# A fixed TensorE order, one plain token tile, spread output products and paired value additions in a local-attention plus gated-MLP block

## The chip, the cores and the metric

The kernel runs on one core of one Trainium2 chip. The metric is the device time of one execution in microseconds (us); when a kernel is compared, several executions of both kernels are taken in turn on the same chip. The engines are called PE (TensorE, matmuls), PEld (the weight loads of TensorE, which overlap its matmuls), DVE (VectorE), ACT (ScalarE), POOL (GpSimd) and SP (SyncE). An engine name with a q (SPq) is that engine's instruction queue; it shows the issue of a transfer, not the transfer itself. L920 is line 920 of the kernel in question, so the same statement has another number in another kernel.

## The reference, cut to what matters

`x` has S = 2048 tokens of 512 features. Two branches read its layernorm. Branch A is attention with 32 heads of 16 features over a window of 8 keys, two tokens apart. Branch B is a gated MLP whose gate mixes tokens with a 2048 x 2048 matrix.

```python
xn = layernorm(x)
# A: 32 heads of 16, window of 8 keys, every second token
q, k, v = split(xn @ wqkv)                       # wqkv 512 x 1536
logits  = sum_d q[s] * k[s - 2*w] * scale        # w = 0..7, masked where s - 2*w < 0
o       = sum_w softmax(logits)[s, w] * v[s - 2*w]
a       = o @ wo                                 # wo 512 x 512
# B: gated MLP with a spatial matrix
z       = gelu(xn @ w_in)                        # w_in 512 x 1792
z1, z2  = z[:, :896], layernorm(z[:, 896:])
g       = w_sp @ z2 + b_sp[:, None]              # w_sp 2048 x 2048
b       = (z1 * g) @ w_out                       # w_out 896 x 512
y       = x + a + b
```

## The kernel before

The program is written as a list of tasks. Each task says what it reads and writes, and a list scheduler in Python, which runs when the kernel is built, puts the tasks of each engine into an order and places the semaphores. The kernel has two stages. In the first 100 us the projections run (q, k, v, z1, z2), DVE multiplies queries with keys, and TensorE sums these products with matmuls against a 0/1 matrix `E8`. In the second stage the spatial product g is computed for four tiles of 512 tokens. For six of seven groups of 128 features it uses seven products of half-size blocks in place of eight (a Winograd form of Strassen's scheme): 256-column matmuls, which need sums of z2 and differences of weights made on DVE. The seventh group is a plain product of 512 columns. Beside this, DVE multiplies attention weights with values and adds them up over the window ("value products"), a transfer transposes the result (`OT`), and TensorE makes the output blocks.

Three kinds of large transfer:

- *Weight transposes*: a DMA transpose of 2 MB of `w_sp` for each token tile, issued by SP, into two slots `wT0` and `wT1`.
- *Value loads*: 1.15 MB (1152 KB in the profile) into one of two buffers `Ve`, issued by POOL, two for each token tile.
- *Output transposes*: small DMA transposes of the attention output from `On` into `OT`, also issued by SP.

Parts, with cuts marked by `...`:

```python
# --- buffers: lay(base, ...) without "base =" starts at the same place as the next line
base = lay(base, ("Sn", 3 * NK * 384))
...
lay(base, ("Ve", 9216), ("wT1", WSL), ("Vs", 4096), ("On", 512), ("xres", 1024), ("yout", 1024), ("wo0", 512))
base = lay(base, ("QT", 4096), ("KT", 8 * (512 + KP)), ("pb", NPB * 4096))
```

So the value buffers lie over queries and keys (and the first part of `pb`), and the second weight slot lies over the products `pb` of the logits: the second weight transpose can start only when the last of these products has been summed.

```python
def prod_reduce(j, c):                       # wave j of 512 tokens, c = 0..3
    ...                                      # DVE: pb[s_] = q * k, 128 x 4096
    if c < 3:
        return
    def mm(t):                               # one piece of 32 matmuls for all four c
        for wh in range(2):
            for cc in range(4):
                sc = (s_ - 3 + cc) % NPB
                for g in range(4):
                    last = t.matmul(PC(32 * g * PR + 3072 + 512 * wh, [[1, 512]], 32),
                                    AC(off["E8"] + 32 * cc, [[1, 32]]),
                                    AC(off["pb"] + 4096 * sc + 2048 * wh + 128 * g, [[512, 4], [1, 128]]),
                                    start=(cc == 0), stop=(cc == 3))
        return last
    T("pe", mm, reads=[("pb", i) for i in range(4)] + ["E8"], writes=["psl"], ...)

def ld_wT(tc, after=()):                     # the weight transpose (L920)
    r_ = tc % 2
    dma("sp", lambda e: e.dma_start_transpose(AC(WT[r_], [[512, NB], [1, 512]]),
        B_w_sp[512 * tc: 512 * tc + 512, :]), 512 * S * 2, ("wT", r_), reads=after,
        writes=[("wB", r_, q) for q in range(4)], name="wT%d" % tc, xbar=True)

def pv_block(b):                             # value products of one block of 128 tokens
    ...
    if q < 2:
        dma("pool", ...)                     # value load into Ve[par] (L1100)
    # DVE: Vs = Ve * attn (4096), then Vs += halves of 2048, 1024, and On = 512 + 512
    ...
    dma("sp", lambda e: e.dma_start_transpose(AC(off["OT"] + 512 * b, [[128, 4], [1, 128]]),
        A("On", 512, 512 * so)), ...)        # the output transpose (L1118)

plain(0); t_sums(0); ld_wT(1)                # written as three lines
for tc in range(NJ):
    for i in range(3):
        prod7(i, tc)                         # seven products, two feature groups each
    for q in qord:
        pv_block(4 * tc + q)
    if tc + 1 < NJ:
        if tc + 2 < NJ:
            ld_wT(tc + 2)
        plain(tc + 1)
        bdiff(tc + 1)
        t_sums(tc + 1)
    for q in qord:
        out_block(4 * tc + q, ...)           # attention part first, then the MLP part
```

Of the kernel before, what the change touches and what calls it, by code (L numbers as in the profile page):

```python
# [9 lines left out]
class Task:  # L10
    __slots__ = ("eng", "fn", "reads", "writes", "est", "name", "dma", "deps", "idx",
                 "start", "end", "eng_end", "count", "tok", "clock", "prio", "tbl", "margin")


class Plan:
# [37 lines left out]
    def add(self, eng, fn, reads=(), writes=(), est=100.0, name="", dma=None, prio=None, tbl=None, margin=0.0):  # L53
# [30 lines left out]
        t.deps = deps  # L84
        for k in t.reads:
            if k not in t.writes:
                self.readers.setdefault(k, []).append(t)
# [6 lines left out]
    def schedule(self, lookahead=64, slack=120.0, dma_bw=300.0, xbar_bw=190.0,  # L94
# [31 lines left out]
        while remaining:  # L126
            best = None
            for e in ENGS:
# [6 lines left out]
                for t in pl:  # L135
                    ok = True
                    ready = 0.0
                    for d in t.deps:
                        if d.end is None:
                            ok = False  # L140
                            break
                        r = d.end + lat(d, t)
                        if r > ready:
                            ready = r
# [66 lines left out]
    def emit(self, nc, block, sems, chan_sems):  # L211
# [32 lines left out]
        def run_engine(e):  # L244
            def body(eng):
                known = {}
                for t in self.order[e]:
                    need = {}
                    dl = [d for d in t.deps if known.get(d.tok[0], 0) < d.tok[1]]
# [57 lines left out]
    fill0=2,  # L307
)


def build_kernel(nc, A_x, A_wqkv, A_wo, B_x, B_w_in, B_w_sp, B_b_sp, B_w_out, out, report=False, sched_kw=None,
# [36 lines left out]
    def lay(base, *items):  # L348
        for name, n in items:
# [6 lines left out]
    base = lay(base, ("Sn", 3 * NK * 384))  # L356
# [4 lines left out]
    lay(base, ("Ve", 9216), ("wT1", WSL), ("Vs", 4096), ("On", 512), ("xres", 1024), ("yout", 1024), ("wo0", 512))  # L361
# [6 lines left out]
               ("bbc", S), ("cb", 2048), ("wo1", 1536))  # L368
    WO = (off["wo0"], off["wo1"], off["wo1"] + 512, off["wo1"] + 1024)
# [15 lines left out]
    with ExitStack() as es:  # L385
# [3 lines left out]
        bdt = es.enter_context(nc.sbuf_tensor("bdt", [128, 512], F32))  # L389
# [33 lines left out]

        def q_off(c, j):
            return off["QT"] + (c * S + 512 * j if not True else 2048 * (j % 2) + 512 * c)
# [11 lines left out]
        for s_ in range(2):  # L437
            R1(("On", s_), "On", 512)
# [10 lines left out]
        R1("Vs", "Vs", 4096)  # L449
        for s_ in range(2):  # L450
# [17 lines left out]
        for b in range(NB):  # L468
            R(("xnT", b), "sb", [(off["xnT"] + dc * S + 128 * b, off["xnT"] + dc * S + 128 * b + 128)
                                 for dc in range(4)])  # L470
            R1(("OT", b), "OT", 512, 512 * b)
            R1(("z2", b), "z2", FH, FH * b)
        R1("w_in1", "w_in1", 4 * FH)
# [24 lines left out]
        def c_dve(n, mode=1.0):  # L498
            return 130.0 + n / (0.96 * mode)

        T = plan.add
# [221 lines left out]
        def prod_reduce(j, c):  # L723
# [9 lines left out]
            if R2:  # L733
                if c < 3:
                    return

                def mm(t):
                    last = None
                    for wh in range(2):
                        for cc in range(4):  # L740
                            sc = (s_ - 3 + cc) % NPB
                            for g in range(4):
                                last = t.matmul(
                                    PC(32 * g * PR + 3072 + 512 * wh, [[1, 512]], 32),
                                    AC(off["E8"] + 32 * cc, [[1, 32]]),
                                    AC(off["pb"] + 4096 * sc + 2048 * wh + 128 * g, [[512, 4], [1, 128]]),
                                    start=(cc == 0), stop=(cc == 3))
                    return last
                T("pe", mm, reads=[("pb", i) for i in range(4)] + ["E8"], writes=["psl"],
                  est=8 * 232.0 + 190, name="red%d" % j, margin=cfg.get("m_red", 800.0))  # L750
                return

            def mm(t):
                last = None
                for blk in range(4):
                    t0, ts = tok(4 * j + blk)
                    for w in range(8):
                        last = t.matmul(ps[:, 3072 + blk * 256 + w * 32 + 8 * c: 3072 + blk * 256 + w * 32 + 8 * c + 8],
                                        AC(off["pb"] + 4096 * s_ + 512 * w + t0 - 512 * j, [[ts, 128]]), E8,
                                        start=True, stop=True)  # L760
                return last
            T("pe", mm, reads=[("pb", s_), "E8"], writes=["psl"], est=32 * 25 + 30, name="red%d_%d" % (j, c),
              margin=cfg.get("m_red", 800.0))

# [90 lines left out]
        def z1_group(fc, j):  # L855
            k = next_bank()
# [41 lines left out]
        def s_sums(k0, k1):  # L898
# [7 lines left out]
            zk = [("z2", b) for b in range(2 * k0, 2 * k1)]  # L906
            a11, a12, a21, a22 = z_(0), z_(FH), z_(384), z_(FH + 384)
            for nm, o_, x_, y_, op, rd, wr in (
                    (1, sn(0), a21, a22, ALU.add, zk, [("Sn", 1, k) for k in range(k0, k1)]),
                    (2, sn(1), sn(0), a11, ALU.subtract, zk + [("Sn", 1, k) for k in range(k0, k1)],  # L910
                     [("Sn", 2, k) for k in range(k0, k1)]),
                    (3, a21, a11, a21, ALU.subtract, [], zk),
                    (4, sn(2), a12, sn(1), ALU.subtract, zk + [("Sn", 2, k) for k in range(k0, k1)],
                     [("Sn", 4, k) for k in range(k0, k1)])):
                T("dve", (lambda o_, x_, y_, op: lambda v: v.tensor_tensor(o_, x_, y_, op))(o_, x_, y_, op),
                  reads=rd, writes=wr, est=c_dve(384 * n, 2.0), name="S%d_%d" % (nm, k0))

        def ld_wT(tc, after=()):
            r_ = tc % 2
            dma("sp", lambda e: e.dma_start_transpose(  # L920
# [18 lines left out]
        for j in range(NJ):  # L939
            bl = range(4 * j, 4 * j + 4)  # L940
            for b in bl:
                if b >= 8:
                    ld_x(b)
            if j == 1:
                ld_win1(after=[("xn", 2)])
            for b in bl:
                ln_block(b)
            if j == 0:
                setup_masks()
                for b in bl:  # L950
                    z2_block(b)
            if j == 1:
# [280 lines left out]
```

## Time and profile before

| Kernel before | value |
|---|---|
| time, median of 3 runs | 275.12 us (272.65 to 275.19) |
| span of the profiled run | 270.6 us |
| PE busy | 233.2 us (86%) |
| DVE busy | 207.4 us (77%) |
| idle PE after 104 us | about 31 us |

The page of the profile gives each engine's busy time, and then the span in 40 equal slices, where a digit is the busy share in tenths. The last strip is the clock that the throttle granted to TensorE, in tenths of full speed.

```profile
PE 233.2 (86%) x1493; PEld 138.7 (51%) x1511; DVE 207.4 (77%) x257; ACT 144.1 (53%) x305; POOL 57.3 (21%) x110
...
PE   6999999999999999998005998289999877999696
...
PEclk9999999999999999999855999989999999999979
```

TensorE is nearly full for the first 19 slices; then there is a hole of two slices, with the granted clock down to a half, and smaller holes to the end. The groups of waits say what ended the idle time of an engine: engine and line, the releaser, the total in us, how often, and the longest.

```profile
PE ps L1020 <- DMA arena<-in_B_w_sp_dram: 16.0, 1, 16.0
...
DVE arena L936 <- DMA arena<-in_B_w_sp_dram: 13.0, 1, 13.0
...
PE ps L1058 <- ACT ps L999: 6.4, 6, 1.4
...
PE ps L1141 <- DMA arena<-arena: 5.2, 1, 5.2
```

TensorE's largest wait, and DVE's, is one single transfer of spatial weights. L1058 are the 256-column matmuls; they wait 6.4 us in all for ACT, which hands one product's sum over to the next (a hand-over, below). L1141 is the attention part of an output block, which waits 5.2 us for an output transpose. The timeline around the large wait has start, duration (of the issue, for a transfer), engine, line and operation, and in brackets the idle time before it:

```profile
110.02 0.60 POOL L1100 DMA_DIRECT2D arena<-vscr  x1 [18.42 <-DVE arena L730]
...
113.59 0.55 POOL L1100 DMA_DIRECT2D arena<-vscr  x1 [2.98 <-PE ps L743]
114.07 17.23 SPq L920 DMA_TRANSPOSE arena<-in_B_w_sp_dram  x1
...
125.27 0.54 POOL L1100 DMA_DIRECT2D arena<-vscr  x1 [10.07 <-DVE arena L1107]
...
136.47 3.71 SPq L1118 DMA_TRANSPOSE arena<-arena  x1
140.22 10.06 SPq L920 DMA_TRANSPOSE arena<-in_B_w_sp_dram  x1
...
145.14 2.34 PE L1020 MATMUL ps<-arena 128*128 128x512 bf16 x5 [16.00 <-DMA arena<-in_B_w_sp_dram]
```

Both value loads of the first token tile and the second weight transpose are issued within 4.1 us, and a third value load follows at 125.27. TensorE gets its weights at 145 us. The times from issue to landing of the three weight transposes after 100 us (L920):

```profile
DMA to landing us min/median/max: 9.5/12.1/30.6
```

The same of the 16 output transposes (L1118):

```profile
DMA to landing us min/median/max: 2.4/3.0/8.7
```

The transpose in the gap is the one that took 30.6 us.

### The profile page before, as it was taken

Reading aid. Unit: us, or ns where it says so; the run is one execution under the profiler, and the core shown is the slowest. Engines: PE = TensorE matmul, PEld = TensorE weight load, DVE = VectorE, ACT = ScalarE, POOL = GpSimd, SP = SyncE. Lnnn points to the kernel's source line nnn. Section 1 sums busy time; section 2 is a strip of 40 time slices with the busy share of each in tenths; the row PEclk is TensorE's granted clock in tenths of the full one; section 3 lists DMA queues with packets and bytes.
Section 4 is the critical chain, followed back from the end, with each engine's and each line's share of the span. In section 5 each row is a group of like instructions: output and inputs, shape, how many; then the busy total and the mean of one; then the engine's idle time right before and its main releaser. Section 6 shows DMA issues by size and latency. Waiting matters only on the chain.

```text
span 270.6 us, 3910 instructions
## 1 busy us (share of the span) xinstructions
PE 233.2 (86%) x1493; PEld 138.7 (51%) x1511; DVE 207.4 (77%) x257; ACT 144.1 (53%) x305; POOL 57.3 (21%) x110
## 2 busy tenths in 40 slices
PE   6999999999999999998005998289999877999696
PEld 2544454454444444787002884048487356578543
DVE  4696897896999899689405899689990999989900
ACT  2796689689898875367100533136344154344323
POOL 4556754506100200200000002220121001320000
PEclk9999999999999999999855999989999999999979
DMA  6997920102190003599999723857982252642021
GB/s 221 358 275 142 249 42 31 49 0 80 30 280 2 0 0 107 211 231 177 127 186 234 170 39 76 235 164 161 273 249 49 77 156 62 208 104 58 19 58 61
DMA packets 59266, 35.53 MB, mean 131 GB/s; under 512 B 49644, under 2 KB 56684, under 8 KB 58224
## 3 DMA queue, kind: packets, MB, share of 16 engines
q1 hardware_dynamic: 53856, 18.29, 32.7%
q0 software_dynamic: 3312, 15.22, 19.3%
q10 hardware_dynamic: 2080, 1.77, 2.0%
q8 instruction: 12, 0.20, 0.3%
q14 instruction: 6, 0.05, 0.1%
HBM read 19.01 MB, written 4.21 MB: 86 GB/s over the span
## 4 chain that ended last, share of the span: by engine, by line
PE 52%; DVE 24%; DMA 17%; issue 3%; ACT 3%; SPq 0%; POOL 0%; DVEq 0%; ACTq 0%
DMA arena<-in_B_w_sp_dram 11%; PE ps L704 10%; PE ps L861 9%; PE ps L844 9%; DVE arena L1107 8%; PE ps L1058 5%; PE ps L684 5%; PE ps L1146 5%; DMA arena<-arena 4%; PE ps L1020 4%; DVE arena L1109 4%; PE ps L1141 3%; DVE arena L936 2%; DVE arena L1112 2%; DVE arena L1079 2%
## 5 line engine op out<-in xcount | busy, mean ns | idle before, releaser
L1058 PE MATMUL ps<-arena 128*128 128x256 bf16 x672 | 75.8, 273 | 6.4 <-ACT ps L999 6.4
L1058 PEld LDWEIGHTS ps<-arena 128*128 128x128 bf16 x672 | 65.1, 98 | 17.7 <-ACT ps L999 8.4
L1107 DVE TENSOR_TENSOR arena<-arena 128x4096 bf16<-128x4096 bf16 x16 | 36.6, 2291 | 1.2 <-DMA arena<-vscr 0.7
L730 DVE TENSOR_TENSOR arena<-arena 128x4096 bf16<-128x4096 bf16 x16 | 35.9, 2278 | 0.0
L936 DVE TENSOR_TENSOR arena<-arena 128x2048 bf16<-128x2048 bf16 x16 | 19.5, 1221 | 21.1 <-DMA arena<-in_B_w_sp_dram 13.0
L999 ACT ACTIVATE arena<-ps 128x256 bf16<-128x256 f32 (+1 forms) x28 | 11.4, 412 | 40.9 <-PE ps L1020 25.1
L1152 ACT ACTIVATE arena<-ps 128x512 bf16<-128x512 f32 (+2 forms) x17 | 9.7, 572 | 43.9 <-PE ps L1146 37.5
L1020 PE MATMUL ps<-arena 128*128 128x512 bf16 x60 | 15.0, 402 | 16.1 <-DMA arena<-in_B_w_sp_dram 16.0
L1146 PE MATMUL ps<-arena 128*128 128x512 bf16 (+2 forms) x119 | 28.5, 382 | 0.0
L704 PE MATMUL ps<-arena 128*128 128x512 bf16 x125 | 28.0, 379 | 0.3 <-ACT arena L871 0.2
L844 PE MATMUL ps<-arena 128*128 128x448 bf16 x128 | 25.7, 353 | 0.9 <-ACT arena L712 0.3
L1141 PE MATMUL ps<-arena 128*128 128x512 bf16 (+2 forms) x63 | 17.0, 393 | 8.9 <-DMA arena<-arena 5.2
L861 PE MATMUL ps<-arena 128*128 128x512 bf16 x109 | 24.2, 379 | 0.2
L1129 POOL DMA_DIRECT2D arena<-in_A_x_dram x16 | 8.6, 538 | 66.1 <-ACT ps L1136 38.2
L1146 PEld LDWEIGHTS ps<-arena 128*128 128x128 bf16 x119 | 13.5, 117 | 13.3 <-issue 3.2
L704 PEld LDWEIGHTS ps<-arena 128*128 128x128 bf16 x128 | 12.4, 98 | 15.3 <-issue 0.4
L1109 DVE TENSOR_TENSOR arena<-arena 128x2048 bf16<-128x2048 bf16 x16 | 19.5, 1221 | 0.4
L999 ACT ACTIVATE ps<-ps 128x256 f32<-128x256 f32 x36 | 13.1, 367 | 12.1 <-PE ps L1058 10.3
L849 ACT ACTIVATE arena<-ps 128x448 bf16<-128x448 f32 x32 | 17.2, 547 | 3.5 <-PE ps L844 1.8
L712 ACT ACTIVATE arena<-ps 128x1024 bf16<-128x1024 f32 x16 | 16.2, 1021 | 5.3 <-PE ps L704 5.3
L844 PEld LDWEIGHTS ps<-arena 128*128 128x128 bf16 x128 | 12.1, 98 | 13.1 <-ACT arena L671 1.0
L1020 PEld LDWEIGHTS ps<-arena 128*128 128x128 bf16 x64 | 6.5, 103 | 23.8 <-DMA arena<-in_B_w_sp_dram 15.9
(75 smaller groups left out, 296.7 us busy)
## 6 DMA issues: line engine op xcount, KB each, us to landing
arena<-vscr POOLq DMA_DIRECT2D x8, 1152.0 KB, 6.5
vscr<-arena POOLq DMA_DIRECT2D x16, 128.0 KB, 3.3
arena<-in_A_x_dram POOLq DMA_DIRECT2D x16, 128.0 KB, 3.3
arena<-in_A_x_dram SPq DMA_DIRECT2D x14, 128.0 KB, 7.3
out_dram<-arena POOLq DMA_DIRECT2D x12, 128.0 KB, 3.8
arena<-in_A_wqkv_dram SPq DMA_DIRECT2D x2, 512.0 KB, 7.9
arena<-in_B_w_in_dram SPq DMA_DIRECT2D x1, 896.0 KB, 7.9
arena<-in_B_w_out_dram SPq DMA_DIRECT2D x1, 896.0 KB, 5.0
```

What stands on the lines that cost most here:

```text
L704: last = t.matmul(bank(k + which), AC(off["wqk"] + 1024 * dc + col0, [[1, 128]]), AC(off["xnT"] + dc * S + 512 * j, [[1, 512]]), start=(dc ...
L730: T("dve", lambda v: v.tensor_tensor(pbv, qb, kb, ALU.mult), reads=rd, writes=[("pb", s_)], est=c_dve(4096, 2.0), name="prod%d_%d" % (j, c ...
L844: last = t.matmul(ps[:, 512 * k: 512 * k + HF], AC(off["xnT"] + dc * S + 128 * b, [[1, 128]]), AC(off["w_in2"] + FH * dc + c0, [[1, HF]]), ...
L861: lastm = t.matmul(bank(k), AC(off["w_in1"] + FH * dc + 128 * fc, [[1, 128]]), AC(off["xnT"] + dc * S + 512 * j, [[1, 512]]), start=(dc == ...
L936: T("dve", (lambda o_, x_, y_: lambda v: v.tensor_tensor(o_, x_, y_, ALU.subtract))(o_, x_, y_), reads=rd, writes=[wr], est=c_dve(NK * 256 ...
L999: T("act", lambda a: a.activation(out_, in_, ACTF.Copy), reads=reads, writes=writes, est=c_act(n), name=name)
L1020: last = t.matmul(bank(k), AC(off["z2"] + FH * sh + 128 * fc, [[1, 128]]), AC(WT[r_] + sh * 512, [[1, 512]]), start=False, stop=(sh == NB ...
L1058: last = t.matmul(half(bk), lh(k), rh(k), start=False, stop=(k == NK - 1), skip_group_check=True)
L1107: T("dve", lambda v: v.tensor_tensor(tv, iv, av, ALU.mult), reads=[("attn", j)] + rdv, writes=["Vs"], est=c_dve(4096, 2.0), name="pv%d" % ...
L1109: T("dve", lambda v: v.tensor_tensor(A("Vs", 2048), A("Vs", 2048), A("Vs", 2048, 2048), ALU.add), writes=["Vs"], est=c_dve(2048, 2.0), nam ...
L1141: t.matmul(po, AC(off["OT"] + 512 * tb + 128 * cc, [[1, 128]]), AC(WO[cc] + c0, [[1, n]]), start=False, stop=False, skip_group_check=True)
L1146: last = t.matmul(po, AC(off["z1T"] + fc * S + t0, [[ts, 128]]), AC(off["w_out"] + 512 * fc + c0, [[1, n]]), start=False, stop=(fc == FC - ...
```

## The change

The change writes TensorE's order by hand instead of leaving it to the scheduler (only the reductions of the logits and the transposes of x stay with the scheduler). The first token tile uses plain products only, so that its weights' differences and sums need not be made and there is work for TensorE while the second weights come. Output blocks and the plain products of the next tile are cut into slices that are placed in the gaps between the seven products. The value products of two blocks share their additions. The reduction of the logits becomes four pieces, the order of the projection waves changes, the value buffers get space of their own, output blocks do their MLP part first, output and residual transfers move from POOL's queue to ACT's, SP's transposes get a fixed order too, TensorE no longer waits on semaphores for its own earlier matmuls, the products read z2 by parts instead of as a whole, all of `wo` gets space of its own, and banks and scheduler constants change.

The core of the diff, with cuts marked:

```diff
+    def sequence(self, tasks):
+        for a, b in zip(tasks, tasks[1:]):
+            b.odeps.add(a)
...
-    def schedule(self, lookahead=64, slack=120.0, dma_bw=300.0, xbar_bw=190.0,
+    def schedule(self, lookahead=400, slack=120.0, dma_bw=300.0, xbar_bw=400.0,
...
-    base = lay(base, ("Sn", 3 * NK * 384))
-    lay(base, ("Ve", 9216), ("wT1", WSL), ("Vs", 4096), ("On", 512), ("xres", 1024), ("yout", 1024), ("wo0", 512))
+    base = lay(base, ("Ve", 9216))
+    lay(base, ("Sn", 3 * NK * 384), ("wT1", WSL), ("Vs", 4096), ("On", 1024), ("xres", 1024), ("yout", 1024))
...
-                T("pe", mm, reads=[("pb", i) for i in range(4)] + ["E8"], writes=["psl"],
-                  est=8 * 232.0 + 190, name="red%d" % j, margin=cfg.get("m_red", 800.0))
+                T("pe", mm, reads=[("pb", s_), "E8"], writes=["psl"],
+                  est=2 * 232.0 + 100, name="red%d_%d" % (j, c), margin=cfg.get("m_red", 800.0))
...
-            P(1, X, za(0), wb(0), z2all + [("wB", r_, 0)])
+            P(1, X, za(0), wb(0), za11 + [("wB", r_, 0)])
+            gap()
...                                            # two more gap() in each prod7
+        def pv_pair(j, par):
...
+            for n, nm in ((2048, "a"), (1024, "b"), (512, "c")):
+                o_ = two(0, n) if n > 512 else AC(off["On"], [[512, 2], [1, 512]])
+                T("dve", (lambda o_, n: lambda v: v.tensor_tensor(o_, two(0, n), two(n, n), ALU.add))(o_, n),
+                  reads=[] if n > 512 else ["Vs", ("Ve", par)], writes=["Vs", ("Ve", par)] if n > 512 else ["On"], ...)
+            return dma("sp", lambda e: e.dma_start_transpose(AC(off["OT"] + 2048 * j + 1024 * par, [[128, 8], [1, 128]]),
+                                                             A("On", 1024)), ...)
...
         for tc in range(NJ):
+            if tc == 0 and P0:                 # P0 = cfg["first_plain"]
+                for fc in (3, 4, 5, 0, 1, 2, 6):
+                    for n_, f_ in plain_slices(0, next_bank, (16,), fc):
+                        f_()
+                for n_, f_ in plain_slices(1, next_bank, (16,)):
+                    f_()
...
+            else:
+                pl = plain_slices(tc + 1, ob) if tc + 1 < NJ else []
+                oq = [out_slices(4 * (tc - 1) + q) for q in qord] if tc > 0 else [[], [], [], []]
+                q_ = oq[0] + oq[1] + pl + oq[2] + oq[3]
...                                            # gap() takes its share of q_
+                for i in range(3):
+                    prod7(i, tc, gap)
+            for par in range(2):
+                if tc > 0:
+                    ld_V(tc, par)
+                sp_seq.append(pv_pair(tc, par))
+                if par == 0 and tc + 2 < NJ:
+                    sp_seq.append(ld_wT(tc + 2))
...
+        plan.sequence(pe_seq)
+        plan.sequence(sp_seq)
```

## The prediction

> **What bounds the kernel now.** PE is 233.2 of 270.6 us busy (page; 86%), DVE 207.4 (77%). In the view by stretches PE is busy 96.5 of the first 100 us: the projections are PE-bound. After they end, at 104 us, PE idles 31 us, nearly all in waits:
> - 129.1 to 145.1 us: 16.0 us for the second token tile's spatial-weight transpose (groups of waits; DVE 13.0). It was issued only at 114.07: its space overlays the logits' product buffers, freed by the reduction at 113.2. Two value loads of 1.15 MB were issued at 110.0 and 113.6. It took 30.6 us to land; the median of the four is 10.9. After it seven matmuls start 0.43 us apart instead of 0.22: 1.5 us more. The Trainium skill, "TensorE: Matmul & The Clock Gate", Part 1, says that an idle TensorE drops to half clock; this trace agrees (granted clock 0.65 in the gap).
> - 5.2 us for a transposed attention output (170 to 175 us), then 4.5 us at 210-233 and 2.3 us before 256.9, where DVE is late; the chain runs on DVE from 210 to 256 us.
>
> **What changes.**
> - Tile 0 uses plain products: 168 matmuls of 256 columns out (measured pitch 0.110 us, 18.5 us), 96 of 512 in (0.216 us, 20.7 us): PE +2.3 us. DVE loses four weight differences (4 x 1.22) and three merges and multiplies (3 x 1.37), gains six multiplies of 0.42: -6.5 us.
> - Value products: additions of two blocks share an instruction; per pair 2 x (1.22+0.69+0.42) = 4.7 becomes 2.3+1.22+0.69 = 4.2 us (estimate); 8 pairs: -3.8 us.
> - Value buffers get their own space, so tile 0's loads go early, away from the weight transpose. That can go about 20 us earlier, and TensorE has 128 plain matmuls (27.7 us) to hide it.
> - Output and plain matmuls between the seven products cover ScalarE's 0.38 us hand-overs, which now stall PE 6.4 us in all. Output DMAs move from Pool to ACT, which has room (53%).
>
> **Sum.** The plain stage should start at about 107 us: 104.3, plus the fourth reduction (1.9), which came later before, plus small waits for the logits' products, which DVE must finish some 10 us earlier. Then 27.7 + 504 x 0.110 (55.4) + 32 x 0.216 (6.9) + 176 x 0.216 (38.0) = 128 us: 235 us. I add 5 us of waits where DVE (about 197 us in all) and PE run neck and neck, and 3 us for the last store: span 243. The reported time is 2 to 4 us above the span (272.3 against 270.6; median 275.1). I predict 246 us, 8 in 10 between 239 and 256: 10.5% faster. On the critical path: 17.5 us from the late transpose, some 10 from outputs and DVE waits. Chances: faster by over 2% 0.97, same 0.02, slower 0.01.
>
> **What would show it.** No PE wait over 3 us on spatial weights; second weight transpose issued before 100 us, landing in under 20; PE busy above 93%, its clock 1.0 from 10 us on; DVE about 197 us; a chain mostly PE; pair addition 2.3 us.
>
> **What would make it wrong.** TensorE's order is fixed, so one late operand stops everything behind it: logits' products late on DVE (PE waits at the 32-row matmuls), weight differences of tiles 1 to 3 late (waits at the 256-wide matmuls), or ACT evictions held behind a DMA waiting in its queue. The pair addition could lose its rate (over 3 us).

## The result

The kernel after takes 252.03 us (median of 4 runs, 249.21 to 253.45); the kernel before took 274.31 us in the runs beside it (272.65 to 275.19, 4 runs). The ratio is 0.9125, with a 95% interval of 0.9021 to 0.9229. Ratios in this document are the mean time of one kernel's fast runs over that of the other's fast runs of the same rounds, so they are not quite the ratio of the medians that are quoted beside them. Against the quick mode of the kernel before, which turns up in the experiments below (mean 264.6 us), the kernel after is about 5% faster (251.05 us in the second set). The 246.0 that was predicted is 6 us too low; the range of 239 to 256 holds the result.

The profiled run took 253.04 us. It is called slow by the rule that a run more than 1.5% above the kernel's fastest is slow (it is 1.54% above), but the four runs (249.21, 251.03, 253.04, 253.45) are a spread without a gap. A second trace of the same kernel from the second set of experiments (250.57 us) shows the same waits with other sizes, and is quoted beside it.

The page after, same parts:

```profile
PE 235.3 (94%) x1413; PEld 130.6 (52%) x1439; DVE 195.6 (78%) x228; ACT 142.6 (57%) x293; POOL 48.5 (19%) x82
...
PE   8799998999999999999999983999799989999994
...
PEclk9999999999999999999999996899999999999999
```

PE is busy as long as before, in a span that is 19 us shorter. One deep hole is left, in the 25th slice, with a lower clock behind it. The waits after:

```profile
DVE arena L1144 <- DMA arena<-arena: 10.9, 2, 6.1
...
PE ps L1042 <- DMA arena<-in_B_w_sp_dram: 4.8, 1, 4.8
...
PE ps L1187 <- DVE arena L1118: 1.4, 1, 1.4
```

The wait for spatial weights went from 16.0 to 4.8 us, and it is for another tile: the third, not the second. The output matmuls (L1187) no longer wait for an output transpose. In exchange DVE waits 10.9 us for output transposes before its paired additions (L1144), because they write the one buffer `On` that the transpose still reads. The timeline around the hole shows how this comes about:

```profile
116.29 1.25 SPq L1147 DMA_TRANSPOSE arena<-arena  x1
...
116.49 0.60 POOL L1124 DMA_DIRECT2D arena<-vscr  x1 [21.89 <-DVE arena L1144]
...
134.88 13.11 SPq L933 DMA_TRANSPOSE arena<-in_B_w_sp_dram  x1
138.17 0.55 POOL L1124 DMA_DIRECT2D arena<-vscr  x1 [21.08 <-DVE arena L1144]
148.03 10.16 SPq L1147 DMA_TRANSPOSE arena<-arena  x2
154.82 1.46 PE L1042 MATMUL ps<-arena 128*128 128x512 bf16 x3 [4.78 <-DMA arena<-in_B_w_sp_dram]
156.24 0.69 DVE L1144 TENSOR_TENSOR arena<-arena 128x1024 bf16<-128x1024 bf16 x1 [6.07 <-DMA arena<-arena]
```

The last paired addition releases the output transpose (116.29) and the next value load (116.49) in the same moment. They run against each other, and the output transpose took 12.1 us to land. The third weight transpose was issued at 134.88 and a value load at 138.17; the transpose landed after 19.9 us, at 154.8, and the next matmul in TensorE's fixed order needed it. From issue to landing, the four weight transposes (L933) of the kernel after took:

```profile
DMA to landing us min/median/max: 10.0/11.9/19.9
```

And its eight output transposes (L1147):

```profile
DMA to landing us min/median/max: 3.9/6.9/14.0
```

The median of the output transposes was 3.0 us before and is 6.9 after (each now carries two blocks). In the second trace the third weight transpose took 18.5 us, PE waited 3.4 us for it, and DVE waited 11.1 us for output transposes.

### The profile page after: what moved, and what is told of

Read it like the earlier page. It is cut to its first block, busy times and chain, and to the rows that moved or that the text cites. A ratio compares the mean times of both kernels' runs of the same rounds, so it can differ in the third digit from the quotient of the medians.

```text
span 251.3 us, 3687 instructions
## 1 busy us (share of the span) xinstructions
PE 235.3 (94%) x1413; PEld 130.6 (52%) x1439; DVE 195.6 (78%) x228; ACT 142.6 (57%) x293; POOL 48.5 (19%) x82
## 4 chain that ended last, share of the span: by engine, by line
PE 61%; DMA 16%; DVE 14%; ACT 4%; issue 2%; ACTq 1%; SPq 1%; POOL 0%; DVEq 0%
PE ps L1088 11%; PE ps L1042 11%; PE ps L869 10%; PE ps L852 9%; DMA arena<-in_B_w_sp_dram 8%; PE ps L1187 7%; PE ps L729 6%; DVE arena L1135 4%; DVE arena L1144 3%; PE ps L763 3%; PE ps L709 3%; DMA arena<-in_B_w_in_dram 3%; DMA arena<-in_B_b_sp_dram 2%; DMA arena<-arena 2%; DVE arena L949 2%
## 5 line engine op out<-in xcount | busy, mean ns | idle before, releaser
L1088 PE MATMUL ps<-arena 128*128 128x256 bf16 x504 | 61.2, 277 | 1.0 <-ACT ps L1015 0.8
L1088 PEld LDWEIGHTS ps<-arena 128*128 128x128 bf16 x504 | 50.0, 99 | 13.5 <-ACT ps L1015 1.1
L1015 ACT ACTIVATE arena<-ps 128x512 bf16<-128x512 f32 (+3 forms) x45 | 22.5, 501 | 41.7 <-PE ps L1042 14.5
L1144 DVE TENSOR_TENSOR arena<-arena 128x4096 bf16<-128x4096 bf16 (+2 forms) x24 | 33.6, 1400 | 11.6 <-DMA arena<-arena 10.9
L1187 PE MATMUL ps<-arena 128*128 128x512 bf16 (+2 forms) x177 | 40.4, 366 | 1.8 <-DVE arena L1118 1.4
L1042 PE MATMUL ps<-arena 128*128 128x512 bf16 x154 | 35.7, 384 | 5.0 <-DMA arena<-in_B_w_sp_dram 4.8
L729 PE MATMUL ps<-arena 128*128 128x512 bf16 x123 | 28.4, 379 | 0.4 <-issue 0.2
L1042 PEld LDWEIGHTS ps<-arena 128*128 128x128 bf16 x160 | 15.7, 99 | 23.4 <-DMA arena<-in_B_w_sp_dram 5.3
L1187 PEld LDWEIGHTS ps<-arena 128*128 128x128 bf16 x187 | 19.5, 108 | 15.5 <-DVE arena L1118 1.7
L869 PE MATMUL ps<-arena 128*128 128x512 bf16 x109 | 24.5, 379 | 0.3 <-issue 0.2
L1124 POOL DMA_DIRECT2D arena<-vscr x8 | 4.4, 554 | 104.4 <-DVE arena L1144 101.9
L1015 ACT ACTIVATE ps<-arena 128x512 f32<-128x512 bf16 (+3 forms) x36 | 19.0, 534 | 7.6 <-DMA arena<-in_A_x_dram 3.7
L729 PEld LDWEIGHTS ps<-arena 128*128 128x128 bf16 x128 | 12.0, 98 | 16.1 <-issue 1.7
L852 PEld LDWEIGHTS ps<-arena 128*128 128x128 bf16 x128 | 11.8, 98 | 14.6 <-issue 2.1
L874 ACT ACTIVATE arena<-ps 128x512 bf16<-128x512 f32 x28 | 15.9, 600 | 5.1 <-PE ps L869 4.9
L1015 ACT ACTIVATE ps<-ps 128x256 f32<-128x256 f32 x27 | 9.9, 365 | 14.6 <-PE ps L1088 11.1
L869 PEld LDWEIGHTS ps<-arena 128*128 128x128 bf16 x112 | 10.6, 98 | 13.9 <-issue 0.8
```

The lines of the kernel that those rows point to most:

```text
L729: last = t.matmul(bank(k + which), AC(off["wqk"] + 1024 * dc + col0, [[1, 128]]), AC(off["xnT"] + dc * S + 512 * j, [[1, 512]]), start=(dc ...
L852: last = t.matmul(ps[:, 512 * k: 512 * k + HF], AC(off["xnT"] + dc * S + 128 * b, [[1, 128]]), AC(off["w_in2"] + FH * dc + c0, [[1, HF]]), ...
L869: lastm = t.matmul(bank(k), AC(off["w_in1"] + FH * dc + 128 * fc, [[1, 128]]), AC(off["xnT"] + dc * S + 512 * j, [[1, 512]]), start=(dc == ...
L1015: T("act", lambda a: a.activation(out_, in_, ACTF.Copy), reads=reads, writes=writes, est=c_act(n), name=name)
L1042: last = t.matmul(bank(k), AC(off["z2"] + FH * sh + 128 * fc, [[1, 128]]), AC(WT[r_] + sh * 512, [[1, 512]]), start=False, stop=(sh == NB ...
L1088: last = t.matmul(half(bk), lh(k), rh(k), start=False, stop=(k == NK - 1), skip_group_check=True)
```

## The experiments

Twelve kernels ran in three sets, each set on one chip, and each set beside seven runs of the kernel before. Every run gave the reference's result. The theories of the first set were these. The main theory was that the gain comes from ending a collision: a weight transpose is slow when value loads run beside it. Its rivals were that the gain comes from issuing the second weights earlier or from the plain work that hides them, and that spreading the output products (so covering the hand-overs on ACT) is a gain of its own.

One thing about the kernel before has to be said first. In these sets 15 of its 21 runs took 270.9 to 274.0 us, and 6 took 262.1 to 266.8 us (mean 264.6), with nothing in between. The rule calls the first group slow and uses only the second for ratios. I call them the usual mode and the quick mode. All four runs beside the result above were in the usual mode, and so is the only trace of the kernel before. Where a ratio below is against the quick mode, this is said.

### First set: does the collision of transfers matter, or does a part of the change?

**Before, with the first tile's value loads held back until the second weights have landed (`b_vehold`).**

```diff
-  ... reads=[("vscr", i) for i in range(4 * j - 1, 4 * j + 4)],
+  ... reads=[("vscr", i) for i in range(4 * j - 1, 4 * j + 4)] + ([("wB", 1, 0)] if j == 0 else []),
```

> The kernel before, with one edit: the two value loads of tile 0 (1.15 MB each) wait until the second weight transpose has landed. Theory A (the 30.6 us of that transpose are contention with the value loads, and its late issue alone would have cost little): it lands within 15 us of its issue at about 114 us, the 16.0 us wait of the plain matmuls falls under 3 us, and the time falls by 8 to 15 us. Rival B (the transpose is slow for another reason, or its late issue is what counts): it still takes over 25 us, PE still waits over 10 us, and the time stays within 2%.

Measured: 270.94 us (268.39 to 271.93, 4 runs), 1.8 us (under 1%) less than the median of before (272.70) where 8 to 15 us were expected, and 1.0286 of its quick mode (1.0137 to 1.0435). The second weight transpose, freed of value loads, landed in 13.2 us instead of 30.6, and TensorE's wait for it was gone. But the held loads now ran beside the third one:

```profile
114.95 9.66 SPq L920 DMA_TRANSPOSE arena<-in_B_w_sp_dram  x1
...
129.18 20.60 SPq L920 DMA_TRANSPOSE arena<-in_B_w_sp_dram  x1
131.90 1.06 POOL L1100 DMA_DIRECT2D arena<-vscr  x2
...
162.92 1.49 PE L1141 MATMUL ps<-arena 128*128 128x512 bf16 x3 [17.13 <-DMA arena<-arena]
```

SP needed 20.6 us to issue it where the free one took 9.7, it landed after 24.9 us, and PE waited 17.1 us in one piece for an output transpose instead. That output transpose was not slow itself (2.4 us): it was issued only at 160.0 us, because the held value loads, in flight with the third weights, landed at 149.5 and 152.3. So the mechanism is shown and the expected gain is not: the collision moved from one transfer to the next, and the holding made the values late.

**Before, with a plain first tile and nothing else (`b_plain`).**

```diff
-        plain(0)
-        t_sums(0)
+        for i_, fc in enumerate((3, 4, 5, 0, 1, 2, 6)):
+            plain(0, fc, (0, 1, 3, 4, 5)[i_ % 5])
+        s_sums(0, 8, (3,))
...
-            for i in range(3):
+            for i in range(3 if tc else 0):
                 prod7(i, tc)
```

> The kernel before, with tile 0 alone made plain (96 matmuls of 512 columns for 168 of 256, no weight differences, no merges for tile 0); layout and scheduler as before. Theory A (the gain of the change is not the plain tile as such but the earlier issue of the second weight transpose and its separation from the value loads): the transpose is still issued near 113 us and lands near 140; PE still waits over 8 us; the time is within 2% of before. Rival B (27.7 us of plain matmuls hide the transpose by themselves): the wait is under 3 us and the time falls by over 10 us.

Measured: 262.38 us (261.37 to 269.63, three quick runs and one slow), 0.9963 of the quick mode of before (0.9833 to 1.0092). In a trace of a quick run TensorE no longer waits for the second weights, which came after 17.4 us; the third took 22.3 us, beside a value load. It looks like 10 us gained against the usual mode and like nothing against the quick one, and fits neither theory cleanly.

**After, with the first tile back to seven products (`a_nofirst`).**

```diff
-    first_plain=1,
+    first_plain=0,
```

> The changed kernel with tile 0 by seven products again (a switch in it), all else kept. Theory A: PE has 2.3 us less work, DVE 6.5 us more, and the sums for tile 0 come at about 115 us, just when TensorE needs them: between 3 us faster and 4 us slower than the changed kernel (ratio to before 0.90 to 0.93), with no wait over 3 us on spatial weights of tile 1. Rival B (the plain first tile carries the gain): PE waits over 6 us for tile 0's sums or the second weight tile, and 6 us or more of the 22 are lost (ratio to before over 0.935).

Measured: 259.85 us (256.62 to 268.95, 5 runs), about 8 us slower than the kernel after (252.03 in its own rounds). The trace is of the slowest run (268.95). There the fourth weight transpose took 29.2 us beside a value load, PE waited 14.5 us for it, and DVE 20.8 us for output transposes. I do not explain the median by this trace; it shows again which waits make a slow run.

**After, without spreading: the slices run behind the seven products (`a_nospread`).**

```diff
                     state["gaps"] += 1
+                    if state["gaps"] <= 9:
+                        return
...
                     prod7(i, tc, gap)
+                gap()
```

> The changed kernel with output and plain matmuls behind the three groups of seven products, not between them. Theory A: ScalarE's hand-overs are mostly covered by the products in between (0.87 us of matmuls for a 0.38 us copy and its semaphores), so PE waits for ACT rise from about 1 to 4 us or so: 2 to 5 us slower than the changed kernel (ratio to before 0.92 to 0.93). Rival B (spreading is what the change lives from): over 6 us slower, PE waits for ACT over 6 us.

Measured: 271.41 us (269.99 to 272.61, 4 runs), about 20 us slower than the kernel after and as slow as the one before. Taken at its word, this would make spreading worth 20 us. The trace says otherwise: the last two weight transposes took 20.0 and 40.4 us, DVE waited 27.1 us for output transposes (18.4 in one piece), and much of the 20.2 us that PE waited for ACT at the seven products came from DVE behind it: ACT's own waits for DVE were up to 12.2 us long. The order of TensorE's work had moved the moments at which transfers are issued, and they met more often. A part cannot be valued here while the transfers collide.

### Second set: the parts again, with the transfers kept apart

**The changed kernel once more (`after_again`)**, without an edit, as the measure for this set.

> The changed kernel unaltered, for a second trace and for times beside the runs below on one chip: 249 to 254 us. The third weight transpose, issued near 135 us, meets the value load issued some 3 us later and takes near 20 us again; TensorE waits 4 to 6 us for it.

Measured: 251.05 us (249.95 to 252.64, 4 runs), beside 272.40 for before (usual mode in six runs of seven).

**After, with the large transfers kept apart (`a_clean`).** A value load waits until the output transpose of its pair has landed; the second load of tiles 1 and 2 also waits for the weights in flight, and a weight transpose waits for the value load in flight. `On` gets a second buffer in space that is dead by then. TensorE's order is the same.

```diff
-        R1("On", "On", 1024)
+        R1(("On", 0), "On", 1024)
+        R1(("On", 1), "Za", 1024)
...
             for par in range(2):
-                if tc > 0:
-                    ld_V(tc, par)
                 sp_seq.append(pv_pair(tc, par))
+                if tc + 1 < NJ:
+                    ld_V(tc + 1, par, [("OT", 4 * tc + par)] + ([("wB", tc % 2, 0)] if par and tc + 2 < NJ else []))
                 if par == 0 and tc + 2 < NJ:
-                    sp_seq.append(ld_wT(tc + 2))
+                    sp_seq.append(ld_wT(tc + 2, [("Ve", 0)]))
```

> The changed kernel with its large transfers kept apart: a value load of a later tile waits for the output transpose of the same half to land, the second loads of tiles 1 and 2 also for the weight transpose in flight, a weight transpose for the value load in flight; the transposed output has two buffers. Same instructions on PE, DVE and ACT. Theory C (what remains is contention of the transposes with the value loads): every weight transpose lands within 13 us, output transposes within 5, the 4.8 us PE wait and the DVE's 10.9 us wait for output transposes fall under 1.5 us each, and the time falls by 4 to 8 us against the changed kernel on this chip. Rival D (these waits are slack, something else would stop TensorE in their place): within 2 us of the changed kernel.

Measured: 244.21 us (244.16 to 244.62, 4 runs), which is 6.8 us less than the kernel after in the same set; the means of the four runs each have a ratio of 0.973 (244.30 over 251.17). The spread fell from 2.7 to 0.5 us. The times from issue to landing of all four weight transposes (L934):

```profile
DMA to landing us min/median/max: 10.1/11.1/12.6
```

The same of all eight output transposes (L1148):

```profile
DMA to landing us min/median/max: 3.0/3.2/4.8
```

And the page:

```profile
PE 232.4 (96%) x1413; PEld 129.1 (53%) x1439; DVE 195.4 (81%) x228; ACT 142.4 (59%) x293; POOL 48.1 (20%) x82
...
PEclk9999999999999999999999999999999999999999
```

No transpose takes long any more, no wait of PE is over 1.5 us, and the clock is full throughout. DVE still waits: instead of 10.9 us for output transposes it waits 11.7 us (4.4 and 7.3) at the second value product of a pair (L1136) until the weights in flight have landed. This product writes into the value buffer, and the new rule has made the weight transpose a reader of that buffer. The chain that ended last passes through both waits, so the rule has a price of its own. The busy time of PE is 2.9 us less than in the trace of the kernel after, with the same number of matmuls; no slice shows a lower clock any more, which fits this. So in the changed kernel the collisions and the single `On` cost 6.8 us together, after the price of the rule; this run does not divide it between the two.

**The same without spreading (`a_clean_nospread`)** is `a_clean` with the edit of `a_nospread` on top.

> The same separation of transfers, with output and plain matmuls behind the seven products of a tile. Theory C (the earlier run without spreading lost 20 us mostly because its third and fourth weight transposes met value loads, 20 and 40 us to land, not because of ScalarE hand-overs): 2 to 7 us slower than the kernel with transfers apart and spread. Rival B (spreading itself is worth over 10 us): more than 10 us slower.

Measured: 244.96 us (244.59 to 245.25, 4 runs). Spreading is worth 0.75 us here, not 20, and not the 2 to 7 that were expected.

**The same without the plain first tile (`a_clean_nofirst`)** is `a_clean` with `first_plain=0`.

> The same separation of transfers, with tile 0 by seven products. Theory C (the plain first tile only gives the sums and transposes time; PE 2.3 us less work, DVE 6.5 us more): between 2 us faster and 5 us slower than the kernel with transfers apart and tile 0 plain. Rival B (the plain first tile carries the gain): over 6 us slower.

Measured: 244.94 us (244.73 to 245.31, 4 runs). The plain first tile is worth 0.73 us here, not 8. Both differences are only 0.3%, and they are net of DVE's wait for weights that the rule brings (11.7 us in `a_clean`, 8.6 without spreading, 3.5 without the plain tile). So they show only that neither part is worth the 20 or 8 us of the first set.

### Third set: then what makes the kernel faster?

**Before, with the transfers kept apart (`b_clean`).**

```diff
-  ... reads=[("vscr", i) for i in range(4 * j - 1, 4 * j + 4)],
+  ... reads=[("vscr", i) for i in range(4 * j - 1, 4 * j + 4)] + ([("wB", 1 - j, 0)] if j < 2 else []),
...
-                    ld_wT(tc + 2)
+                    ld_wT(tc + 2, [("Ve", 0), ("Ve", 1)])
```

> The kernel before, with its large transfers kept apart and nothing else: tile 0's value loads wait for the second weight transpose, the third weight transpose for them, tile 1's value loads for the third. Theory C (contention of transposes with value loads is most of the difference; the scheduler, the seven products of tile 0 and the single value products are not): the second weight transpose lands within 14 us, PE waits under 3 us for spatial weights, the two-humped times of before (262 to 274) close up, and the median lies at 252 to 260 us. Rival E (the hand order and the early issue carry it): over 262 us.

Measured: 263.33 us (261.35 to 264.42, 4 runs), 8.5 us less than the median of before (271.83), and 0.9917 of its quick mode (0.9764 to 1.0071), so no different from that. The two modes closed up to one, at the place of the quick one. No weight transpose took over 13.2 us. Keeping transfers apart is thus worth 8.5 us against the usual mode, and leaves 19 us to `a_clean` (of another set), which the collisions do not explain. The 252 to 260 us that were expected if contention is most of the difference were missed: by its own terms the result falls to the rival, that the order or the early issue carries the gain. The next runs try the order.

**The transfers kept apart, and the named parts off (`a_clean_none`)**: `a_clean` without the plain first tile, without spreading and without paired additions, but in the fixed TensorE order.

```diff
-    first_plain=1,
+    first_plain=0,
...
-  for n, nm in ((2048, "a"), (1024, "b"), (512, "c")):      # once for a pair of blocks
+  for n, nm in ((2048, "a"), (1024, "b"), (512, "c")):      # once for each block, as before
...                                                          # and the edit of a_nospread
```

> The changed kernel with transfers apart, and three named parts of the change off at once: no spreading, tile 0 by seven products, one block per value addition. TensorE's order stays fixed. Theory C: the named parts together are worth 1 to 5 us once the transfers do not meet: 245 to 249 us. Rival B: over 252 us.

Measured: 246.26 us (245.69 to 248.75, 4 runs), 0.930 of the quick mode of before (0.9160 to 0.9441). All three parts together are worth 2.1 us (against `a_clean` of the second set, on another chip). Single additions need no product in the value buffer, so this kernel is without the wait for weights that the rule puts on `a_clean`, and the parts may be worth somewhat more than that.

**The same with TensorE's order left to the scheduler (`a_clean_free`).**

```diff
-        plan.sequence(pe_seq)
         plan.sequence(sp_seq)
```

> As the run with the three parts off, and the fixed TensorE order off as well, so that the list scheduler orders all engines as in the kernel before. Theory C: still within 4 us of it, 245 to 252 us. Rival E (the hand order carries the gain): over 255 us.

Measured: 241.02 us (240.80 to 241.29, 4 runs), 0.9088 of the quick mode of before (0.8967 to 0.9209). It is the fastest kernel and 10 us faster than the kernel after. The plain first tile, the paired additions and the order by hand are off in it. Spreading is off only in the hand-written list: the output blocks and plain products are still cut into slices, as the change cut them, and the scheduler is free to place these between the seven products, which it does. From 125 to 225 us of the trace TensorE changes 40 times between these three kinds of work, against 11 times in `a_clean_none` (54 in `a_clean`, 12 in the kernel before). The start of the first tile's seven products (L1089) shows it. First `a_clean_none`, where the plain products (L1043) come first and PE then waits for ACT:

```profile
108.42 3.62 PE L1043 MATMUL ps<-arena 128*128 128x512 bf16 x16
113.15 7.16 PE L1089 MATMUL ps<-arena 128*128 128x256 bf16 x64 [1.11 <-ACT ps L1016]
122.06 11.72 PE L1089 MATMUL ps<-arena 128*128 128x256 bf16 x104 [1.75 <-ACT ps L1016]
```

Then `a_clean_free`, where plain products of the next tile stand between them:

```profile
111.89 1.04 PE L1089 MATMUL ps<-arena 128*128 128x256 bf16 x8
112.76 1.03 PE L1043 MATMUL ps<-arena 128*128 128x512 bf16 x4
113.62 1.04 PE L1089 MATMUL ps<-arena 128*128 128x256 bf16 x8
```

PE waits 5.0 us for ACT in the whole of the first trace and 1.6 us in the second. So with the other parts off, the order by hand without spreading is 5.2 us slower than the scheduler's own order with its own spreading; against the hand order with spreading, the plain tile and the pairs (`a_clean`, another set) the free order is 3.2 us faster. That the plain tile, the pairs or the order by hand carry the gain, as the change's title suggests, has failed here. What the cutting into slices is worth under a free order was not tried.

To see where the time between `b_clean` and `a_clean_free` went, both with undisturbed transfers, the stretches of 25 us can be laid side by side. The columns are the stretch, its length, then the busy time of PE, PEld, DVE, ACT and POOL (with the instructions), and the granted clock, the DMA share and GB/s. First `b_clean`:

```profile
0.00:100.00 100.00, 96.44 (x532) 44.20 (x533) 80.90 (x131) 78.60 (x158) 39.06 (x74) 1.00 0.46 119
100.00:125.00 25.00, 24.82 (x202) 17.02 (x199) 16.39 (x14) 14.96 (x31) 1.15 (x2) 1.00 0.53 126
...
175.00:200.00 25.00, 23.59 (x167) 16.39 (x166) 19.83 (x21) 10.24 (x22) 4.31 (x8) 1.00 0.83 225
...
225.00:280.00 55.00, 30.70 (x216) 21.42 (x214) 20.22 (x22) 12.89 (x31) 3.04 (x6) 0.95 0.17 45
```

Then `a_clean_free`:

```profile
0.00:100.00 100.00, 98.27 (x545) 41.94 (x546) 85.23 (x129) 76.46 (x155) 43.23 (x76) 1.00 0.66 163
100.00:125.00 25.00, 24.98 (x164) 15.05 (x163) 24.35 (x27) 15.73 (x29) 0.60 (x1) 1.00 0.45 123
...
175.00:200.00 25.00, 25.00 (x177) 17.40 (x175) 23.27 (x23) 11.46 (x26) 1.05 (x2) 1.00 0.94 219
...
225.00:280.00 55.00, 9.87 (x55) 5.09 (x53) 0.73 (x2) 5.13 (x10) 0.00 (x0) 0.97 0.08 22
```

The two have nearly the same DVE work (207.8 and 205.9 us) and TensorE work (236.4 and 233.1). What differs most is when DVE does it. In `b_clean` DVE still has 20 us of work after 225 us, with PE behind it. In `a_clean_free` it is done: it had worked 4.3 us more in the first 100 us, 8.0 us more in the next 25, and 3.4 us more from 175 to 200. In the second of these stretches `b_clean` has no values to multiply: its two loads of the first tile are issued only at 132 us, while `a_clean_free`, whose `Ve` has its own space, issued them at 31 us. This is in part the price of `b_clean`'s own rule (the kernel before issued them at 110.0 and 113.6): with `Ve` on top of queries and keys, the loads can be kept away from the second weights only by holding them back. So `b_clean` is the kernel before with its collisions removed and a delay put in, and not a clean measure of the collisions alone.

**The reduction of the logits back in one piece (`a_clean_red4`)**: `a_clean` with the reduction as in the kernel before.

```diff
-                T("pe", mm, reads=[("pb", s_), "E8"], writes=["psl"], name="red%d_%d" % (j, c), ...)
+                T("pe", mm, reads=[("pb", i) for i in range(4)] + ["E8"], writes=["psl"], name="red%d" % j, ...)
```

> The changed kernel with transfers apart, and the logits' reduction in one piece of 32 matmuls again instead of four of 8. Measured so far: a piece of 32 takes 1.84 us, four pieces of 8 take 2.2 us together, so PE gains about 1.4 us; but the last reduction, and with it the second weight transpose, comes some 13 us later (about 104 us), and DVE's weight differences wait for it. Expected 242.5 to 246 us; if the early transpose matters for TensorE, over 246.

Measured: 253.43 us (253.15 to 253.53, 4 runs), 0.9551 of the quick mode of before (0.9460 to 0.9641) and 9.2 us above `a_clean`, though of another set. The matmuls themselves got cheaper: from its start to the next matmul's a reduction takes 1.84 us, and four pieces 4 x 0.55 = 2.2 us, so 1.4 us over the four waves, and the plain stage starts at 107.1 us instead of 107.9. But the second weight transpose, which needs the space of the products, went out later and everything after it as well. The value products need this space too (`Vs`); the first of them moved from 100.7 to 107.1 us.

```profile
103.77 10.07 SPq L939 DMA_TRANSPOSE arena<-in_B_w_sp_dram  x1
...
136.80 0.60 POOL L1130 DMA_DIRECT2D arena<-vscr  x1 [50.41 <-DMA arena<-arena]
142.86 8.32 SPq L939 DMA_TRANSPOSE arena<-in_B_w_sp_dram  x1
...
154.37 1.89 PE L1048 MATMUL ps<-arena 128*128 128x512 bf16 x4 [7.73 <-DMA arena<-in_B_w_sp_dram]
```

In this trace and that of `a_clean`: the issue moved from 90.1 us to 103.8, the first output transpose from 113.4 to 133.2, and with it the next value load from 117.4 to 136.8. The third weights, at 142.9 instead of 132.4, came too late for TensorE by 7.7 us. There is a catch: that the third transpose waits for the value load is a rule of `a_clean`, not of the kernel after, so the whole 9.2 us cannot be carried over to that kernel. And `a_clean` is of another set.

## Why the prediction was right or wrong

**The time: right, 6.0 us too low.** The sum was 243 us of span; `a_clean`, which has the instructions of the change and no such collisions, has a span of 242.4 us. (The 2 to 4 us from span to reported time were 1.7.) The sum left out one term, the collisions between transfers that the change itself brings about: 6.8 us (251.05 less 244.21).

**"Plus the fourth reduction (1.9), plus small waits", so a plain stage from 107 us: mis-sized.** It started at 110.5 us, and at 108.3 us in the second trace. Reductions in pieces take 1.4 us more of PE's time over the four waves (2.2 us each against 1.84), which the prediction did not count, because it took a whole reduction (1.9 us) for the four parts. The rest differs between the two traces, which are 2 us apart already at the first value loads (32.4 and 30.5 us). The stage itself was then sized well: predicted 27.7 us, and from 110.5 to 138.3 us (27.8) in the trace.

**"Second weight transpose issued before 100 us, landing in under 20": right in the sizes, wrong in its reason.** It was issued at 92.7 us and landed after 10.0 us. The text joined this to the value buffers' own space. But that transpose still lies over the logits' products, as before; it goes out earlier because the last products and their reduction are earlier. `a_clean_red4` shows that the reduction in pieces carries 13.7 us of this (103.8 less 90.1 us).

**"No PE wait over 3 us on spatial weights" and "its clock 1.0 from 10 us on": wrong.** PE waited 4.8 us, and the mean clock was 0.986. The prediction had read the 30.6 us transpose as slow because of the two loads beside it (it did not see the third, which met it for longest), and applied this only to that transpose. The changed kernel starts an output transpose and a value load on one signal, and a value load 3.3 us after a weight transpose. The wait could have been foreseen from the diff: `pv_pair` ends both holds with its last addition. The Trainium skill, "TensorE: Matmul & The Clock Gate", Part 1, gives half clock after an idle window of about 3.4 us; the trace agrees, with a granted clock of 0.50 from 154.8 to 158.0 us, after the wait of 4.8 us. The page of the Trainium skill "DMA: Bandwidth & Descriptors", section "Queues, rings and completion order", says that each DMA engine takes turns between the queues that have work. The runs agree that transfers of SP and POOL stretch each other, the weight transpose from about 10 us to between 14.5 and 40.4 us where a value load was in flight for over 3 us of it, and the 1.15 MB load from 5.3 to 6.0 us (in `a_clean`, after the first tile) up to 25.2 us (in `a_nospread`).

**"On the critical path: 17.5 us from the late transpose, some 10 from outputs and DVE waits": the wrong step.** The total came true, the shares did not. That the total came true is no proof of the shares: it was summed from TensorE's work, which did fit, and not from what each part saves. Taking the collisions out of the kernel before (`b_clean`) gives 8.5 us, not 17.5. Part of this is the delay that its rule puts in; and PE then waits elsewhere: 6.9 us for ACT's hand-overs, 5.2, 2.3 and 2.2 us at the output matmuls (L1141), and at the end the chain still runs on DVE. "Output and plain matmuls between the seven products cover ScalarE's 0.38 us hand-overs" was true as a local fact (PE's wait for ACT at the seven products fell from 6.4 to 0.8 us), but worth only 0.75 us of time in `a_clean`. The plain tile that "has 128 plain matmuls (27.7 us) to hide" the second weights is worth 0.73 us there, as these come in time without it. In the medians:

| Step | us |
|---|---|
| before, usual mode, third set | 271.8 |
| transfers kept apart, nothing else (`b_clean`) | 263.3 |
| the change with transfers apart, without plain tile and pairs, TensorE's order free (`a_clean_free`) | 241.0 |
| the same with TensorE's order by hand, slices not spread (`a_clean_none`) | 246.3 |
| plus spreading, plain first tile and pairs (`a_clean`, second set) | 244.2 |
| the change as it is, with its collisions (`after_again`, second set) | 251.1 |

So 22.3 us lie between the kernel before with its transfers held apart and the one that has neither the order by hand nor the plain tile nor the pairs, and 17.1 us are left where spreading is off as well (`a_clean_none`). In the traces DVE works earlier; that this is the cause is argued from them and not shown by a run of its own. A part of it is that the hold of `b_clean` is no longer needed, as the value buffers have their own space. The order by hand, without spreading, costs 5.2 us against the scheduler's, the other named parts give 2.1 back (net of the wait that the rule puts on them), and the collisions that came with the change take 6.8 us.

**The costs of the single operations: right.** DVE was to be busy about 197 us and was 195.6; the pair addition was to take 2.3 us and takes 2.289; PE was to be above 93% and was at 94%; the chain was to be mostly PE, and PE has 61% of it, DMA 16% and DVE 14%.

**What stays open.** Why a run of the kernel before falls into the usual or the quick mode was not seen, as no quick run was traced; that `b_clean` has one mode, near the quick one, fits a collision that sometimes happens, but this is argued and not shown. Of the unnamed edits, only the reduction in pieces was undone alone, and in a kernel with added waits. The own space of the value buffers, the order of waves, the MLP part first in the output blocks, the output transfers on ACT's queue, SP's fixed order, TensorE's dropped waits for its own matmuls, the finer tracking of z2 and the scheduler's constants were not separated. The kernels named `a_clean` also have a second `On`, which the change has not. Nor was each named part, the cutting into slices above all, tried alone under a free order.

## What to carry to other kernels

When large transfers run beside each other, an edit anywhere in the schedule changes which of them meet, and its measured time is then that of the meeting: spreading seemed worth 20 us and was worth 0.75. Keep the transfers apart with explicit waits first, then value each part, and try the edits that the title does not mention. An order written by hand should be compared with the scheduler's own order on the same slices; here the scheduler's was 5.2 us faster than an unspread order by hand, as in the traces it put slices where the other waited for ACT. And check in the trace that a part which was switched off is really gone.

## What the Trainium skill lacked or had wrong

- "DMA: Bandwidth & Descriptors", section "Rules for kernel authors", says: "A transpose next to ordinary DMAs needs nothing". This is about correctness, and every run here was correct. Of the time it says nothing, and there the neighbour matters: a 2 MB transpose landed in 9.4 to 14.1 us with no 1.15 MB load of POOL's in flight, and in 14.5 to 40.4 us where one was in flight for over 3 us of it. An output transpose of two blocks took 3.0 to 4.8 us in `a_clean`, and 8.3 to 15.2 us in those kernels and places where such a load was issued within 0.3 us behind it.
- The same page, section "Latency and other measured facts", gives 261 GB/s for one kernel's transpose with a non-contiguous middle dimension. Here 2.10 MB landed in 10.1 to 12.6 us in `a_clean`, which is 166 to 208 GB/s (worked out, with the latency in it). The page's figure is of another kernel, so this may be another case and not an error.
- No page says that the issue of a transpose by SP itself takes longer beside another transfer: SP needed 7.3 to 10.1 us to issue a weight transpose with no value load beside it and up to 26.0 us (in `a_nofirst`) with one, so that small transposes behind it in the queue waited too.
- No page has two time modes of a one-core program: the kernel before took 262 to 267 us in 6 of 21 runs and 271 to 274 us in 15, on each of three chips.
- "TensorE: Matmul & The Clock Gate" has no measured cost for cutting a run of 32-row matmuls into pieces: here 32 matmuls of 512 columns with 32 output rows took 1.84 us in one piece, and 2.2 us in four pieces of 8 that ran apart (4 x 0.55, start to the start of the next matmul).
